# A convolution and two MLPs on one core: second products of two steps together while the weights are decoded

## The chip, the cores and the metric

The kernel runs on one core of a Trainium2 chip. The metric is the device time of one execution in microseconds (us), taken as the median of several runs. Before the change it is 2296.68 us, the median of 3 runs (2296.4 to 2298.99).

## The reference

Three stages over 16384 tokens of 192 channels, cut to what matters:

```python
# x: (4, 4096, 192), 8 heads of 24 channels, a causal convolution of 7 taps per head
w = softmax(weight, axis=-1)
y = einsum('hk,bskhg->bshg', w, windows(x_padded))     # then 16384 x 192
h = y @ w_in1;  g = h * cos(h);         y = g @ w_out1  # 192 -> 2048 -> 192
h = y @ w_in2;  g = where(h > 0, h, exp(min(h, 0)) - 1); out = g @ w_out2
```

The weights of the MLPs come in as 64-bit floats. The kernel reads each as two 32-bit words, low and high, and builds a 32-bit value from them; that is the decoding. Every product is then made from a high and a low part of both factors (h.h, l.h and h.l), so that reduced-precision matmuls give close to single precision.

## The kernel before, in words

**Tiles.** A block is 512 tokens (there are 32), with channels on the partitions. 192 channels are one full set of 128 partitions and one of 64. A step is one block, one MLP (m = 1 or 2) and one index j of 8; it covers 256 of the 2048 hidden channels, as two tiles of 128, i = 0 and 1. There are 512 steps. Blocks go in groups of four: m = 1 over the four blocks (32 steps), then m = 2 over the same four. Blocks 0 and 1 of m = 1 are taken in halves of four steps each, in turn.

**A step's first products (A).** `products_A` (L527) gives 9 matmuls for each of the two tiles of the step; each uses 64 rows of the array. `side_by_side` issues those of the two tiles in turn, so that one works on the upper and one on the lower rows at the same time. The results u go to a ring of four PSUM banks (`ring_bank`, L520): tile t = 2s + i uses bank t mod 4, so step s + 2 writes the banks that step s wrote.

**What becomes of u.** For a tile of m = 1: ScalarE rounds u to an integer (L608), VectorE takes the fraction (L617), ScalarE makes the sine (L623), VectorE multiplies it with u (L631, the last reader of the bank), ScalarE takes the high part gh (L637), GpSimd the low part gl (L644). `step` (L874) writes these in an order by hand: in step s, for t = 2s and then t = 2s + 1, first L608 and L617 of tile t, then L623 and L631 of tile t - 1, then L637 and L644 of tile t - 2, and between them pieces of the decoding, taps of the convolution and evacuations. So L631 of the second tile of step s is issued in step s + 1, behind L608 and L617 of the first tile of step s + 1. Each engine takes its instructions in that order. gh and gl have six buffers each, those of three steps.

**A step's second products (B).** They come LAG = 3 steps later. While the weights are decoded, `whole_B` (L554) makes them as 10 matmuls that use all 128 rows, into two banks, a0 and a1. After that, four banks are free for it and B is made of 20 matmuls of 64 rows, which `products` (L585) issues side by side with those of A. A block keeps the first form when the decoding isn't over at its first B; that is so for the first 32 steps, and their B are issued in steps 3 to 34. PE's order there is A(3) B(0) A(4) B(1) A(5) B(2) and so on.

**Decoding.** The weights of both MLPs come in 30 pieces (`pieces`, L791). Each goes through `decode` (L178) in stages that `advance` (L814) issues: the load into a raw buffer; on ScalarE L195 and for two pieces of three the absolute value, L197; on VectorE L199, for the third piece of three the absolute value instead (L201), then L202 and L203; on GpSimd L205; then the high part on ScalarE and the low part on GpSimd (L233 and L234, or L254 and L255). `need` (L838) issues further stages until what a step's products read is ready. Raw buffers 4 and 5 lie in a tile (`rows`) whose other columns hold the convolution's tap matrices; RAW_FROM says from which step on they may be used.

**The opening.** `opening` (L927) is a generator that runs once after each step. After step 2 it issues the 7 taps of block 2's first 128 channels as matmuls (`conv_by_products`, L398, line L403, into bank a1), ScalarE's copy of them (L940), a transpose on VectorE (L350) and loads. Further taps follow on VectorE, one a step (L376).

Of the kernel before, what the change touches and what calls it, by code (L numbers as in the profile page):

```python
# [12 lines left out]
I32 = mybir.dt.int32  # L13
# [11 lines left out]
PAIR = 4  # L25
AWAKE = 14
AHEAD, AHEAD2 = 6, 5
RAW_FROM = 0, 0, 0, 0, 3, 3
RAW_UNTIL = 9, 13, 23, 30, 15, 15


# [1 line left out]
def conv_then_two_mlps(ctx, tc, x, weight, w_in1, w_out1, w_in2, w_out2, out):  # L33
# [139 lines left out]
        zp = zt.tile([P, 2, N], F32R, tag=f"zp{b % ZN}", name="z")  # L173
        return zp[:, 0], zp[:, 1], zt.tile([P, N], F32R, tag=f"zc{b % ZN}", name="z")

    turn, scalar = deque(("", "e1", "")), deque((0, 1, 1))

    def decode(m, load, n):  # L178

        raw, use = raw_tile(n)
        load(raw)
        yield
        lo, hi = raw[..., 0], raw[..., 1]
        brink.reverse()
        t = brink[0][:, 0:n]
        turn.rotate(-1)  # L190
        w = (op if turn[0] else stage).tile([P, N], F32, tag=turn[0] or "w", name="w")[:, 0:n]
        bits = w.bitcast(I32)
        scalar.rotate(-1)
        size = w if scalar[0] else t
        nc.scalar.activation(out=t, in_=lo.bitcast(U32), func=AF.Copy, scale=2.0 ** -51, bias=2.0)  # L195
        if size is w:
            nc.scalar.activation(out=w, in_=f32(hi), func=AF.Abs)  # L197
        yield
        nc.vector.scalar_tensor_tensor(out=lo, in0=hi, scalar=SIGN, in1=t.bitcast(I32), op0=ALU.bitwise_and, op1=ALU.bitwise_or)  # L199
        if size is t:  # L200
            nc.vector.tensor_scalar(out=t.bitcast(I32), in0=hi, scalar1=~SIGN, scalar2=0, op0=ALU.bitwise_and, op1=ALU.bitwise_or)  # L201
        nc.vector.tensor_scalar(out=t, in0=size, scalar1=2.0 ** -15, scalar2=2.0 ** 17 - 2.0 ** 13, op0=ALU.max, op1=ALU.min)  # L202
        nc.vector.tensor_scalar(out=bits, in0=t.bitcast(I32), scalar1=3, scalar2=0, op0=ALU.logical_shift_left, op1=ALU.bitwise_or)  # L203
        yield
        nc.gpsimd.tensor_tensor(out=bits, in0=bits, in1=lo, op=ALU.add)  # L205
        taken.difference_update(use)
        yield w
# [190 lines left out]
    def conv_by_products(b, o):  # L398


        xT = xTs.pop(("a", b))
        for k in range(K):
            nc.tensor.matmul(o, lhsT=taps[:, k], rhs=xT[:, k * Q:k * Q + N], start=k == 0, stop=k == K - 1)  # L403
            if k == K - 1:
                ys["a", b] = o
            yield
# [130 lines left out]
    def products_B(s, i):  # L537

        m, b, j = steps[s]
        if (m, b) not in acc:  # L540
            acc[m, b] = [bank(k, "acc") for k in ("a0", "b0", "a1", "b1")]
        o, c, p = acc[m, b][i], acc[m, b][2 + i], half[i]
        h, l, sel = (wo[m, n] for n in ("h", "l", "s"))
        ops = []
        for f in (2 * j, 2 * j + 1):
            gh, gl = gs[f"{s} {f % 2}"]
            st, sp = f == 0, f == NF - 1
            for to, w, g, first, final in ((o, l, gh, st, False), (o, h, gh, False, False), (c, sel, gh, st, False), (o, h, gl, False, sp), (c, sel, gl, False, sp)):
                ops.append((to, w[p, f], g[p], first, final))
        if s == total - 1:  # L550
            ops = [ops[n] for n in (2, 4, 7, 0, 1, 9, 3, 5, 6, 8)]
        yield from ops

    def whole_B(s):  # L554

        m, b, j = steps[s]
        begins, stops = (j % (NP // 2) for j in (j, j + 1)) if split_up(m, b) else (j, (j + 1) % NP)
        if not begins:
            acc[m, b] = [bank(k, "acc") for k in ("a0", "a1")]
        o, c = acc[m, b]  # L560
        h, l, sel = (wo[m, n] for n in ("h", "l", "s"))
        (gh0, gl0), (gh1, gl1) = gs[f"{s} 0"], gs[f"{s} 1"]
        f0, f1 = 2 * j, 2 * j + 1
        st, sp = not begins, not stops
        ops = [(o, l, f0, gh0), (o, h, f0, gh0), (c, sel, f0, gh0), (o, l, f1, gh1), (o, h, f1, gh1), (c, sel, f1, gh1), (o, h, f0, gl0), (c, sel, f0, gl0), (o, h, f1, gl1), (c, sel, f1, gl1)]
        for n, (to, w, f, g) in enumerate(ops):
            nc.tensor.matmul(to, lhsT=w[:, f], rhs=g, start=st and n in (0, 2), stop=sp and n >= len(ops) - 2)  # L567
# [6 lines left out]
    def ends_here(m, b, j):  # L574
        return j == NP - 1 or split_up(m, b) and j == NP // 2 - 1

    def side_by_side(*streams):

        for pr in zip_longest(*streams):
            for product in pr:  # L580
                if product:
                    o, lhsT, rhs, first, final = product
                    nc.tensor.matmul(o, lhsT=lhsT, rhs=rhs, start=first, stop=final)  # L583

    def products(s):  # L585
        now, then = 0 <= s < total, 0 <= s - LAG < total
        if then and steps[s - LAG][2] == 0 and not late:
            whole.add(steps[s - LAG][:2])
        if not then or steps[s - LAG][:2] in whole:
            if now:  # L590
                side_by_side(products_A(2 * s), products_A(2 * s + 1))
            if then:
                whole_B(s - LAG)
        elif not now:
            side_by_side(products_B(s - LAG, 0), products_B(s - LAG, 1))
        else:
            streams = products_B(s - LAG, 0), products_B(s - LAG, 1)
            side_by_side(chain(products_A(2 * s), streams[0]), chain(streams[1], products_A(2 * s + 1)))
        if then:
            for i in (0, 1):  # L600
                del gs[f"{s - LAG} {i}"]

    def emit_act1(s):
        m = steps[s // 2][0]
# [269 lines left out]
    def step(s):  # L874
        now = 0 <= s < total
        present[0] = s
        if now:
            m, b, j = steps[s]
            need(m, j + 1, "o", "c")
        finish = iter(())  # L880
        if 0 <= s - LAG < total:
            m, b, j = steps[s - LAG]
            need(m, 2 * j + 2, "oh", "os")
        products(s)
        ends = 0 <= s - LAG < total and ends_here(*steps[s - LAG])
        if ends:
            assert not lazy
            finish = evac(*steps[s - LAG])
        if s in begin_at:
            m, b = begin_at[s]  # L890
            chores.append(begin_split(b) if m == 1 else double_z(b))
        first_mlp = now and steps[s][0] == 1
        for i in (0, 1):
            t = 2 * s + i
            if i:
                next(finish, None)
            if now:
                emit_act1(t)
                emit_mid(t)
            next(finish, None)  # L900
            if 0 <= t - 1 < 2 * total:
                emit_act2(t - 1)
                emit_g(t - 1)
            if not prepared and (s < NP // 2 or i != ends and (s < 12 or not ends and (s % 3 or s > 18))):
                advance()
            if 0 <= t - 2 < 2 * total:
                emit_hi(t - 2)
                emit_lo(t - 2)
            if i:
                next(finish, None)  # L910
            if now and not first_mlp and not ends:
                next(cq, None)
                if i and not first_mlp and steps[s][2] in (4, 6):
                    next(cq, None)
            chore()
        if prepared and not late:
            brief.close()
            top.close()
            late.append(ctx.enter_context(tc.tile_pool(name="ps_s", bufs=1, space=bass.MemoryType.PSUM)))

    total = len(steps)
    def run(gen, n=99):
        for _ in range(n):
            if next(gen, 0) == 0:
                break

    def opening():  # L927

        yield
        fold(1, bank("a1", "y"))  # L930
        upper_split(1)
        run(conv_by_products(1, bank("a0", "y")))
        run(split(1))
        conved.update((0, 1))
        turn_segment("a", 2)
        load_a(3)
        yield
        run(conv_by_products(2, bank("a1", "y")))
        y = kept(2)
        nc.scalar.activation(out=y, in_=ys["a", 2], func=AF.Copy)  # L940
        ys["a", 2] = y
        turn_segment("c", 2)
        load_c(4)
        upper = conv_taps("c", 2, xTs.pop(("c", 2)))
        yield
        yield
        yield
        for s in range(5, 12):
            run(upper, 1)
            yield  # L950
        run(upper)
        moved.add("o")
        conved.add(2)
        yield
        lower = conv("a", 3)
        for _ in range(7):
            run(lower, 1)
            yield
        run(lower)
        conved.add(3)  # L960
        yield
# [79 lines left out]
```

## Time and profile before

| | us |
|---|---|
| median of 3 runs | 2296.68 |
| the profiled execution | 2297.01 |
| its span | 2295.3 |
| PE (TensorE matmul) busy | 2265.7 |
| VectorE busy | 1768.8 |
| ScalarE busy | 1862.8 |
| GpSimd busy | 1253.0 |

The profiled execution's own time is 2297.01 us, 1.7 us more than its span, and 0.33 us over the median. All times inside the trace count from the start of the span. In a row of the trace "[0.56 <-DVE w L631]" means that the engine sat idle for 0.56 us until that instruction of VectorE (DVE) had ended. PE is TensorE, PEld its weight loads, ACT ScalarE, POOL GpSimd.

### The profile page before, as it was taken

What the parts mean: (1) busy time and instruction counts of PE and PEld (TensorE: products, weight loads), DVE (VectorE), ACT (ScalarE), POOL (GpSimd) and SP (SyncE); (2) the same over time, 40 slices, a digit from 0 to 9 for tenths busy, and PEclk for the clock granted to TensorE, in tenths of its full rate; (3) what the DMA queues carried; (4) which work ended last, traced back from release to release, by engine and by line L of the source; (5) the groups of instructions that cost most, each with busy time, mean ns of one, the idle gap of its engine ahead of it and who ended that gap; (6) DMA issues with size and microseconds to landing.
All of it is one profiled execution on the core that took longest, in us unless ns stands there. A gap on an engine that the chain in (4) does not pass through costs nothing.

```text
span 2295.3 us, 49382 instructions
## 1 busy us (share of the span) xinstructions
PE 2265.7 (99%) x19226; PEld 1839.5 (80%) x19226; DVE 1768.8 (77%) x2564; ACT 1862.8 (81%) x3422; POOL 1253.0 (55%) x975
## 2 busy tenths in 40 slices
PE   8999999999999999999999999999999999999998
PEld 5667888888888888888888888888888888888887
DVE  7986977779777897778967798676986779777655
ACT  6877788888888788888788888888788887888886
POOL 5895335763367533674446743576435763367532
PEclk9999999999999999999999999999999999999999
DMA  7222221213211132112221123212221113211111
GB/s 167 81 68 49 51 58 36 46 32 64 49 36 38 32 69 48 40 29 57 52 52 33 24 58 55 47 38 44 45 57 35 46 34 64 42 36 38 26 38 22
DMA packets 292603, 111.43 MB, mean 49 GB/s; under 512 B 245840, under 2 KB 260176, under 8 KB 292368
## 3 DMA queue, kind: packets, MB, share of 16 engines
q1 hardware_dynamic: 290048, 107.42, 22.4%
q8 instruction: 150, 2.46, 0.4%
q10 hardware_dynamic: 2320, 0.85, 0.2%
q14 instruction: 85, 0.70, 0.1%
HBM read 30.09 MB, written 12.58 MB: 19 GB/s over the span
## 4 chain that ended last, share of the span: by engine, by line
PE 89%; DVE 8%; issue 1%; ACT 1%; DMA 1%; POOL 0%; ACTq 0%; DVEq 0%; SPq 0%; POOLq 0%
PE acc L583 45%; PE u L583 42%; DVE y L376 1%; PE acc L567 1%; DVE w L633 1%; DVE w L631 1%; DVE w L617 1%; DVE gl L644 1%; DVE t L202 1%; DVE w L203 0%; DMA raw<-in_moe_w_in_dram 0%; DMA raw<-in_moe_w_out_dram 0%; DVE y L374 0%; DVE raw L199 0%; PE y L403 0%
## 5 line engine op out<-in xcount | busy, mean ns | idle before, releaser
L644 POOL TENSOR_TENSOR gl<-w,gh 128x512 fp32r<-128x512 f32 x768 | 1013.7, 1321 | 1001.8 <-ACT gh L637 640.0
L583 PE MATMUL acc<-gh,wo_hl 64*128 64x512 f32 x3840 | 1174.3, 386 | 0.0
L583 PEld LDWEIGHTS acc<-gh,wo_hl 64*128 64x128 f32 x3840 | 705.3, 184 | 75.8 <-DVE z L697 0.4
L583 PE MATMUL acc<-gh,wo_s 64*128 64x512 f32 x1920 | 740.8, 386 | 0.0
L583 PE MATMUL acc<-gl,wo_hl 64*128 64x512 f32 x1920 | 740.2, 386 | 0.0
L583 PE MATMUL acc<-gl,wo_s 64*128 64x512 f32 x1920 | 740.1, 386 | 0.0
L637 ACT ACTIVATE gh<-w 128x512 fp32r<-128x512 f32 x1024 | 641.2, 626 | 16.2 <-DVE w L633 15.8
L583 PE MATMUL u<-ch,wi_c 64*128 64x512 f32 x2048 | 619.4, 391 | 14.1 <-DVE w L631 11.4
L583 PE MATMUL u<-sh,wi_o 64*128 64x512 f32 x2048 | 611.4, 387 | 0.0
L617 DVE SCALAR_TENSOR_TENSOR w<-u,w 128x512 f32<-128x512 f32 x512 | 352.0, 687 | 251.1 <-ACT w L608 249.1
L633 DVE SCALAR_TENSOR_TENSOR w<-w,u 128x512 f32<-128x512 f32 x512 | 347.8, 679 | 215.1 <-ACT w L625 210.0
L610 ACT ACTIVATE w<-u 128x512 f32<-128x512 f32 x512 | 306.2, 598 | 186.7 <-PE u L583 167.1
L608 ACT ACTIVATE w<-u 128x512 int32<-128x512 f32 x512 | 306.4, 598 | 184.2 <-PE u L583 178.5
L583 PE MATMUL u<-z,wi_o 64*128 64x512 f32 x1536 | 427.4, 386 | 0.0
L583 PEld LDWEIGHTS u<-ch,wi_c 64*128 64x128 f32 x2048 | 364.7, 184 | 71.7 <-DVE w L631 18.9
L583 PEld LDWEIGHTS u<-sh,wi_o 64*128 64x128 f32 x2048 | 368.5, 185 | 40.7
L583 PE MATMUL u<-sl,wi_o 64*128 64x512 f32 x1024 | 387.1, 387 | 0.0
L583 PE MATMUL u<-cl,wi_c 64*128 64x512 f32 x1024 | 386.7, 387 | 0.0
L583 PEld LDWEIGHTS acc<-gh,wo_s 64*128 64x128 f32 x1920 | 353.3, 184 | 37.9 <-DVE e L698 0.3
L583 PEld LDWEIGHTS acc<-gl,wo_hl 64*128 64x128 f32 x1920 | 353.3, 184 | 37.6
L583 PEld LDWEIGHTS acc<-gl,wo_s 64*128 64x128 f32 x1920 | 353.2, 184 | 37.6
L631 DVE TENSOR_TENSOR w<-u,w 128x512 f32<-128x512 f32 x512 | 348.8, 681 | 41.4 <-ACT w L623 41.4
(143 smaller groups left out, 3608.2 us busy)
## 6 DMA issues: line engine op xcount, KB each, us to landing
out_dram<-e SPq DMA_DIRECT2D x189, 64.0 KB, 2.0
xa<-in_x_dram SPq DMA_DIRECT2D x124, 88.0 KB, 2.9
sh<-z SPq DMA_DIRECT2D x64, 128.0 KB, 2.9
sl<-z SPq DMA_DIRECT2D x64, 128.0 KB, 2.5
ch<-z SPq DMA_DIRECT2D x64, 128.0 KB, 2.4
cl<-z SPq DMA_DIRECT2D x64, 128.0 KB, 2.4
sh<-xh SPq DMA_DIRECT2D x62, 128.0 KB, 2.3
sl<-xl SPq DMA_DIRECT2D x62, 128.0 KB, 2.3
```

Of the source, the lines that this page charges most:

```text
L202: nc.vector.tensor_scalar(out=t, in0=size, scalar1=2.0 ** -15, scalar2=2.0 ** 17 - 2.0 ** 13, op0=ALU.max, op1=ALU.min)
L376: nc.vector.scalar_tensor_tensor(out=o, in0=i, scalar=w, in1=o, op0=ALU.mult, op1=ALU.add)
L567: nc.tensor.matmul(to, lhsT=w[:, f], rhs=g, start=st and n in (0, 2), stop=sp and n >= len(ops) - 2)
L583: nc.tensor.matmul(o, lhsT=lhsT, rhs=rhs, start=first, stop=final)
L608: nc.scalar.activation(out=w.bitcast(I32), in_=u, func=AF.Copy, bias=0.25)
L610: nc.scalar.activation(out=w, in_=u, func=AF.Relu, scale=-1.0)
L617: nc.vector.scalar_tensor_tensor(out=w, in0=u, scalar=0.25, in1=w.bitcast(I32), op0=ALU.add, op1=ALU.subtract)
L631: nc.vector.tensor_tensor(out=w, in0=u, in1=w, op=ALU.mult)
L633: nc.vector.scalar_tensor_tensor(out=w, in0=w, scalar=-1.0, in1=u, op0=ALU.add, op1=ALU.max)
L637: nc.scalar.activation(out=gh, in_=wrk[t], func=AF.Copy)
L644: eng.tensor_tensor(out=gl, in0=wrk.pop(t), in1=f32(own[0]), op=ALU.subtract)
```

## The change

Four edits. The B of a step in the first form are no longer issued in each step, but those of two steps together in every other one: `due` gives nothing where s - 3 is even, and steps s - 4 and s - 3 where it is odd. The order on PE becomes A(3) A(4) B(0) B(1) A(5) A(6) B(2) B(3) and so on; the order on the other engines follows the same rule as before. Every absolute value of the decoding is made by ScalarE. Of block 2's taps as matmuls, three are issued after step 2 and four after step 3, with what follows them. Raw buffers 4 and 5 are used from step 4 on instead of step 3.

```diff
-RAW_FROM = 0, 0, 0, 0, 3, 3
+RAW_FROM = 0, 0, 0, 0, 4, 4
...
-    turn, scalar = deque(("", "e1", "")), deque((0, 1, 1))
+    turn = deque(("", "e1", ""))
...
-        scalar.rotate(-1)
-        size = w if scalar[0] else t
         nc.scalar.activation(out=t, in_=lo.bitcast(U32), func=AF.Copy, scale=2.0 ** -51, bias=2.0)
-        if size is w:
-            nc.scalar.activation(out=w, in_=f32(hi), func=AF.Abs)
+        nc.scalar.activation(out=w, in_=f32(hi), func=AF.Abs)
         yield
         nc.vector.scalar_tensor_tensor(out=lo, in0=hi, scalar=SIGN, in1=t.bitcast(I32), op0=ALU.bitwise_and, op1=ALU.bitwise_or)
-        if size is t:
-            nc.vector.tensor_scalar(out=t.bitcast(I32), in0=hi, scalar1=~SIGN, scalar2=0, op0=ALU.bitwise_and, op1=ALU.bitwise_or)
-        nc.vector.tensor_scalar(out=t, in0=size, scalar1=2.0 ** -15, scalar2=2.0 ** 17 - 2.0 ** 13, op0=ALU.max, op1=ALU.min)
+        nc.vector.tensor_scalar(out=t, in0=w, scalar1=2.0 ** -15, scalar2=2.0 ** 17 - 2.0 ** 13, op0=ALU.max, op1=ALU.min)
...
-    def products(s):
-        now, then = 0 <= s < total, 0 <= s - LAG < total
-        if then and steps[s - LAG][2] == 0 and not late:
-            whole.add(steps[s - LAG][:2])
-        if not then or steps[s - LAG][:2] in whole:
+    def is_whole(s):
+        if steps[s][2] == 0 and not late:
+            whole.add(steps[s][:2])
+        return steps[s][:2] in whole
+
+    def due(s):
+
+        if not 0 <= s - LAG < total:
+            return []
+        if not is_whole(s - LAG):
+            return [s - LAG]
+        return [s - LAG - 1, s - LAG] if (s - LAG) % 2 else []
+
+    def products(s, then):
+        now = 0 <= s < total
+        if not then or is_whole(then[0]):
             if now:
                 side_by_side(products_A(2 * s), products_A(2 * s + 1))
-            if then:
-                whole_B(s - LAG)
+            for k in then:
+                whole_B(k)
...
-        if 0 <= s - LAG < total:
-            m, b, j = steps[s - LAG]
+        then = due(s)
+        for k in then:
+            m, b, j = steps[k]
             need(m, 2 * j + 2, "oh", "os")
-        products(s)
-        ends = 0 <= s - LAG < total and ends_here(*steps[s - LAG])
+        products(s, then)
+        ends = bool(then) and ends_here(*steps[s - LAG])
...
-        run(conv_by_products(2, bank("a1", "y")))
+        lower = conv_by_products(2, bank("a1", "y"))
+        run(lower, 3)
+        yield
+        run(lower)
         y = kept(2)
         nc.scalar.activation(out=y, in_=ys["a", 2], func=AF.Copy)
         ys["a", 2] = y
         turn_segment("c", 2)
         load_c(4)
         upper = conv_taps("c", 2, xTs.pop(("c", 2)))
         yield
         yield
-        yield
```

## Rows read from the trace of the kernel before

**Rows 1.** The page, busy time: span; engine, busy us (share), instructions.

```profile
span 2295.3 us, 49382 instructions
PE 2265.7 (99%) x19226; PEld 1839.5 (80%) x19226; DVE 1768.8 (77%) x2564; ACT 1862.8 (81%) x3422; POOL 1253.0 (55%) x975
```

**Rows 2.** Stretches: sum; busy us (x count) of PE, PEld, DVE, ACT, POOL; PEclk, DMA, GB/s.

```profile
44.90:54.48 9.58, 9.58 (x58) 6.82 (x57) 6.23 (x10) 7.22 (x15) 4.26 (x5) 1.00 0.94 215
54.48:101.38 46.90, 42.48 (x226) 29.49 (x225) 45.72 (x69) 40.67 (x76) 44.11 (x34) 0.96 0.35 92
101.38:158.60 57.22, 52.52 (x281) 36.13 (x280) 52.56 (x75) 44.67 (x83) 47.25 (x36) 0.97 0.27 67
158.60:192.79 34.19, 31.02 (x169) 21.41 (x168) 25.59 (x40) 26.63 (x51) 28.61 (x23) 1.00 0.27 70
192.79:221.51 28.72, 28.72 (x169) 20.45 (x169) 16.85 (x24) 20.70 (x39) 17.42 (x15) 1.00 0.24 50
230.00:2290.00 2060.00, 2055.32 (x18118) 1696.44 (x18114) 1578.90 (x2267) 1691.08 (x3093) 1086.05 (x817) 1.00 0.21 44
```

**Rows 3.** PE's waits from 48 to 222 us: total, times, longest.

```profile
PE u L583 <- DVE w L631: 11.4, 13, 1.8
```

**Rows 4.** Timeline, steps 30 and 31: start, length, engine, line, operation, what it waited for.

```profile
197.58 0.73 PE L583 MATMUL u<-ch,wi_c 64*128 64x512 f32 x4
...
199.85 0.73 PE L567 MATMUL acc<-gh,wo_hl 128*128 128x512 f32 x2
200.01 0.60 ACT L608 ACTIVATE w<-u 128x512 int32<-128x512 f32 x1 [1.62 <-PE u L583]
...
200.50 0.62 ACT L623 ACTIVATE w<-w 128x512 f32<-128x512 f32 x1
200.64 0.69 DVE L617 SCALAR_TENSOR_TENSOR w<-u,w 128x512 f32<-128x512 f32 x1 [1.97 <-ACT w L608]
...
201.25 0.68 DVE L631 TENSOR_TENSOR w<-u,w 128x512 f32<-128x512 f32 x1
...
201.81 0.40 PE L567 MATMUL acc<-gl,wo_hl 128*128 128x512 f32 x1
...
202.04 0.40 PE L567 MATMUL acc<-gl,wo_s 128*128 128x512 f32 x1
...
202.36 0.50 PE L583 MATMUL u<-ch,wi_c 64*128 64x512 f32 x2
```

**Rows 5.** Timeline of PE, where it waited longest inside a step's first products.

```profile
54.48 0.50 PE L583 MATMUL u<-ch,wi_c 64*128 64x512 f32 x1
56.75 0.73 PE L583 MATMUL u<-ch,wi_c 64*128 64x512 f32 x3 [1.77 <-DVE w L631]
...
114.12 0.73 PE L583 MATMUL u<-ch,wi_c 64*128 64x512 f32 x3 [1.62 <-DVE w L631]
...
136.10 0.80 PE L583 MATMUL u<-ch,wi_c 64*128 64x512 f32 x3 [1.52 <-DVE w L631]
...
160.80 0.73 PE L583 MATMUL u<-ch,wi_c 64*128 64x512 f32 x3 [1.69 <-DVE w L631]
```

**Rows 6.** Busy time in two stretches of low granted clock; columns as in Rows 2.

```profile
58.00:61.50 3.50, 3.50 (x13) 2.34 (x10) 3.16 (x5) 2.37 (x5) 2.88 (x4) 0.52 0.51 124
136.60:140.00 3.40, 3.40 (x16) 2.17 (x15) 3.40 (x5) 1.17 (x3) 3.10 (x3) 0.50 0.02 5
```

**Rows 7.** Timeline around the opening, steps 2 and 3.

```profile
38.70 6.28 PE L403 MATMUL y<-spare,rows 128*128 128x512 f32 x14 [2.54 <-DVE spare L350]
...
43.57 0.90 DVE L350 STREAM_TRANSPOSE spare<-xc 128x704 f32<-128x704 f32 x1
...
44.90 0.73 PE L583 MATMUL u<-ch,wi_c 64*128 64x512 f32 x4
```

**Rows 8.** Groups of the decoding, 54.48 to 221.51 us: count, busy, mean ns, idle before.

```profile
L197 ACT ACTIVATE w<-raw 128x512 f32<-128x512 f32 x7 | 4.7, 670 | 0.0
...
L201 DVE TENSOR_SCALAR t<-raw 128x512 int32<-128x512 int32 x4 | 2.8, 695 | 0.1
```

More of the change, by code (lines that the diff above doesn't have):

```diff
@@ L583, in side_by_side @@
                     nc.tensor.matmul(o, lhsT=lhsT, rhs=rhs, start=first, stop=final)
-    def products(s):
-        now, then = 0 <= s < total, 0 <= s - LAG < total
-        if then and steps[s - LAG][2] == 0 and not late:
-            whole.add(steps[s - LAG][:2])
-        if not then or steps[s - LAG][:2] in whole:
+    def is_whole(s):
[11 more added lines that the diff above has]
+        if not then or is_whole(then[0]):
             if now:
                 side_by_side(products_A(2 * s), products_A(2 * s + 1))
-            if then:
-                whole_B(s - LAG)
+            for k in then:
+                whole_B(k)
         elif not now:
-            side_by_side(products_B(s - LAG, 0), products_B(s - LAG, 1))
+            side_by_side(products_B(then[0], 0), products_B(then[0], 1))
         else:
-            streams = products_B(s - LAG, 0), products_B(s - LAG, 1)
+            streams = products_B(then[0], 0), products_B(then[0], 1)
             side_by_side(chain(products_A(2 * s), streams[0]), chain(streams[1], products_A(2 * s + 1)))
-        if then:
+        for k in then:
             for i in (0, 1):
-                del gs[f"{s - LAG} {i}"]
+                del gs[f"{k} {i}"]
     def emit_act1(s):
@@ L880, in step @@
         finish = iter(())
-        if 0 <= s - LAG < total:
-            m, b, j = steps[s - LAG]
+        then = due(s)
+        for k in then:
+            m, b, j = steps[k]
             need(m, 2 * j + 2, "oh", "os")
-        products(s)
-        ends = 0 <= s - LAG < total and ends_here(*steps[s - LAG])
+        products(s, then)
+        ends = bool(then) and ends_here(*steps[s - LAG])
         if ends:
```

## The prediction

> **What bounds the kernel now.** I begin with busy time by engine: PE is busy for 99% of the span [rows 1]. That is an average over two very different parts, so next come the stretches [rows 2]. From 230 us on PE is busy for 2055 of 2060 us and nothing in the change touches that part: what is lost or won before 222 us arrives at the end one to one. The change acts only on steps 3 to 34, on PE from 44.90 us, the first product of step 3, to 221.51 us, the first of step 35. I cut them at the first products of steps 5, 13, 23, 29 and 35. In the last stretch (steps 29 to 34) PE has no holes: 28.72 us for six steps, 4.79 us a step. In the three before it PE idles: 46.90 us for 8 steps (5.86 each), 57.22 for 10 (5.72), 34.19 for 6 (5.70). VectorE is busy for 45.72 of 46.90 us and GpSimd for 44.11 in the first of these, VectorE for 52.56 of 57.22 in the second. So the decode steps are held by VectorE, with GpSimd close behind. The table of waits says how PE feels it: it waited 13 times, 11.4 us in all, for L631 [rows 3], the last reader of the PSUM bank that the next first product writes. That is the edge to follow.
>
> **Pairing B: what it saves.** In steps 30 and 31 [rows 4] A takes 199.85 - 197.58 = 2.27 us and B 202.36 - 199.85 = 2.51 us. A is 9 slots (two matmuls of 64 rows at a time), B 10 slots, and the last two of B start 0.23 us apart (201.81, 202.04). So 2.27 - 9 x 0.23 = 0.20 us of A and 2.51 - 10 x 0.23 = 0.21 us of B are no slot. Each change of form therefore costs about 0.2 us. Two steps have four changes now and two afterwards: 0.4 us saved per pair, 16 pairs, some 6 us if nothing else moved.
>
> **Pairing B: what it uncovers.** Now follow the bank. A(s+2) writes the banks of A(s). Its second matmul needs L631 of the second tile of step s, which is written in step s+1 behind L608 and L617 of that step's first tile. So it can't run before A(s+1) has ended and three more instructions have. The timeline shows this chain free of other work [rows 4]: A(30) gives way to B at 199.85; L608 starts at 200.01, L623 (behind it on ScalarE) at 200.50, L617 at 200.64, L631 at 201.25, and it ends at 201.93. That is 2.08 us after A's end; for the handover to PE I add an estimate of 0.06 us, between those of 0.03 us (end of L608, 200.61, to L617) and 0.13 us (end of L623, 201.12, to L631) in these rows, and take 2.14 us. Today B, 2.51 us, lies exactly over it. After the change every even step's A follows directly on an odd step's A, with nothing in between: PE stands for 2.14 us in each pair. Behind that wait on PE's queue are the rest of A and both B, so all of them are late; ScalarE and VectorE in turn wait for A.
>
> A pair (A odd, hole, A even, B, B) is then 2.27 + 2.14 + 2.16 (A from its second matmul, half a slot less) + 2.30 (ten slots) + 2.51 = 11.38 us, say 11.40. Against 2 x 4.79 = 9.57 us where PE alone is the limit: 1.83 us worse per pair. In the decode stretches against 11.73, 11.44 and 11.40 us. The sum over the 15 pairs of steps 5 to 34: 15 x 11.40 = 171.0 against 167.03 us now, **+4.0 us**. It holds if the other engines' work fits into 11.40 us, below.
>
> **The absolute values.** Six L201 lie in these stretches, 0.695 us each ([rows 8] have four of them; the other two are of the same length), three between 54 and 101 us: 2.1 us. VectorE's 45.72 us become 43.6 against 4 x 11.40 = 45.6; the second stretch has 51.2 against 57.0. ScalarE takes six L197 of 0.670 more; its 40.67 become 42.7 in 45.6. So the swap buys room that the hole then takes; its worth on the path is about nothing. If the hole weren't there it would be worth up to 4.2 us. GpSimd keeps its 44.11 us, and with 45.6 available it is the tightest. I count no extra for engines this full; the bound on the other side is 0.5 us in each of the nine decode pairs, +4.5 us.
>
> **The taps.** 14 matmul records of L403 take 6.28 us, 0.90 us a tap [rows 7]. Four taps after A(3) instead of before it: A(3) starts 3.6 us earlier, at 41.3 us. The four taps, 3.6 us, then lie over the 2.14 us chain, so A(4) sees no hole: it starts at 41.4 + 2.27 + 3.6 = 47.2, B(0) and B(1) run from 49.5 to 54.3, and A(5) starts at 54.3 against 54.48. The transpose of 0.90 us moves behind step 3's VectorE work, with the loads that SP issues after it; VectorE starts step 3 some 3.5 us sooner, so both are covered. Worth -0.2 us on PE's clock position; bounds -2 (VectorE's head start lasts) and +1.
>
> **Raw buffers, evacuation, order of the decoding.** Two pieces load a step later; worked through piece by piece, each is still loaded a step or more ahead of its use, and the decoding ends three steps later than before but ahead of step 35. Nothing; if that failed a whole block more would stay in the first form, but there are over three steps of room. An evacuation of a0 and a1 now has a whole A and a hole more before the next B, so it can only be less late. gh and gl are reused right behind the B that reads them: in an even step L637 must wait for the third matmul of the first B, 0.9 us after A, while L608 and L623 in front of it end 1.3 us after A. Nothing.
>
> **The clock.** A hole costs more than its length when the granted clock falls. The timeline has PE's four longest waits of this kind, 1.52 to 1.77 us of idle time [rows 5]. After the ones that ended at 56.75 and 136.10 the clock fell to half, 1.2 GHz, for 3.4 us [rows 6]; after those of 114.12 and 160.80 it stayed at 2.4 GHz. Two in four. A stretch of 3.4 us at half speed loses 1.7 us of matmuls; today most of that vanishes under VectorE's work. My hole, counted as those are (after the one matmul that goes ahead), is some 1.7 us of idle time: the same kind. With two in four, 7 of 15 holes would cost 1.6 us each, as PE, by then the limit, works on through A and two B: **+11 us**. Bounds: none (0) to all (15 x 1.6 = 24 us).
>
> The Trainium skill has this pattern in "TensorE: Matmul & The Clock Gate", section "A second HAM failure mode: psum-queue depth-cycling": a kernel that cycles through PSUM banks idles briefly between groups of matmuls, and the clock swings between its two levels. By it, nearly each hole would be followed by a slow stretch; this trace agrees in two of four.
>
> **The sum.** -0.2 + 4.0 + 11.2 = +15 us: 2297.0 + 15 = 2312 for the profiled execution, and as the median is 0.33 us lower, about 2311.5 us.
>
> **The rivals.**
> 1. *Hole without the clock*: the waits come as worked out, the granted clock stays at its upper level. +4 us, up to +8 with crowded engines: 2301 to 2305. For it: two of the four rows. Chance 0.24.
> 2. *Every hole drops the clock*: 4 + 24 = +28 us, 2325. For it: from the first matmul of A to the second my hole has 2.25 us, as the one that the clock fell after had (54.48 to 56.75, 2.27) [rows 5]. Against it: the two rows without a fall. Chance 0.10.
> 3. *The hole is shorter than it looks, and the change is faster.* Place: the second matmul of every even A; it decides at 1.88 us, where a pair equals the present mean of 167.03 / 15 = 11.14 us. At half, 1.07 us, a pair has 10.33 us; VectorE would hold the first two stretches at 43.6 and 51.2 us, and six pairs make 62.0: 156.8 against 167.0, -10 us, 2286. For it: PE's 13 waits for L631 average 0.9 us. Against it: each of those had a B in front. Chance 0.10.
> 4. *The edits cancel or the pairing does little*: within 4 us either way. Only 32 of 512 steps are touched. Chance 0.08.
>
> **How the numbers follow.** The forecast (holes, with the clock falling after some) has 0.48, the rivals 0.24, 0.10, 0.10 and 0.08. From 2300 to 2326 us the range holds the forecast, nearly all of rivals 1 and 2, and leaves out 3 and 4. About 0.2%, 4.6 us, is what a measurement of this kernel can tell from no change; slower by more is the forecast, rival 2 and most of rival 1: 0.77. Within it: rival 4 and the low end of rival 1, 0.13. Faster: 0.10.
>
> **What would show it.** In the changed kernel PE's waits for L631 between 48 and 226 us should rise from 11.4 us to some 26 us, about 15 of them, in every second A, and with them steps 29 to 34 should take 34 us or more instead of 28.72. The granted clock should be under 0.95 over that stage. L201 is gone, and VectorE's busy share falls below 0.9 there. Step 3's first product stands near 41.3 us. If steps 29 to 34 take under 28.7 us the chain that I read [rows 4] is wrong; if they take 34 and the clock stays at 1.00, the clock term is.

## The result, and the profile after

The changed kernel takes 2320.38 us, the median of 4 runs (2316.46 to 2323.12), against 2297.3 us for the kernel before (4 runs, 2296.4 to 2298.99). The ratio is 1.0098, with a 95% interval of 1.0081 to 1.0116: slower by 23 us. The direction is the one forecast; with 14.8 us predicted, the size was forecast too small. The profiled execution took 2320.98 us, 24.0 us over that of the kernel before.

The line numbers have moved: A is now issued at L578 (it was L583), B at L562 (L567), and the chain behind u is L614, L623, L629, L637, L643 (it was L608, L617, L623, L631, L637). L639 is the last reader of the bank for m = 2.

The page, busy time and granted clock in 40 slices:

```profile
span 2319.3 us, 49394 instructions
...
PE 2271.5 (98%) x19226; PEld 1875.0 (81%) x19226; DVE 1765.9 (76%) x2554; ACT 1866.5 (80%) x3432; POOL 1251.8 (54%) x975
...
PEclk9998999999999999999999999999999999999999
```

The clock row has an 8 in the fourth slice, which the kernel before didn't have. Busy time of the engines by the same cuts, at the first products of steps 5, 13, 23 and 29 (columns as in [rows 2]):

```profile
54.11:103.09 48.98, 41.64 (x226) 30.28 (x226) 42.87 (x63) 39.73 (x75) 42.55 (x33) 0.93 0.39 101
103.09:168.73 65.64, 53.93 (x281) 39.45 (x280) 51.37 (x72) 45.89 (x85) 48.80 (x38) 0.90 0.24 56
168.73:208.53 39.80, 33.47 (x169) 24.41 (x168) 22.10 (x34) 26.51 (x49) 24.67 (x20) 0.87 0.24 64
208.53:245.97 37.44, 31.94 (x169) 23.26 (x168) 19.43 (x27) 21.28 (x39) 18.04 (x15) 0.91 0.18 38
```

The four stretches have grown from 46.90, 57.22, 34.19 and 28.72 us [rows 2] to 48.98, 65.64, 39.80 and 37.44: 24.8 us together, and that covers the whole loss of 24.0 us. Step 35 begins at 245.97 us and not at 221.51. The clock is at 0.87 to 0.93, where it was 0.96 to 1.00. VectorE, which was busy for 97% of the first of these stretches, is busy for 88% of it now, and for 52% of the last (59% before).

PE's waits from 48 to 246 us (total, times, longest):

```profile
PE u L578 <- DVE w L637: 29.1, 14, 3.5
PE u L578 <- DVE w L639: 1.8, 1, 1.8
```

Fifteen waits, one in each pair, 30.9 us in all, where there were 13 of 11.4 us [rows 3]. The row of m = 2 is the last pair's. This idle time of PE, between the first and the second matmul of an even step's A, is called the hole below. The timeline of one of them, between the first products of steps 29 and 30:

```profile
210.72 0.39 PE L578 MATMUL u<-ch,wi_c 64*128 64x512 f32 x1
210.98 0.60 ACT L614 ACTIVATE w<-u 128x512 int32<-128x512 f32 x1 [2.46 <-PE u L578]
211.47 0.62 ACT L629 ACTIVATE w<-w 128x512 f32<-128x512 f32 x1
211.61 0.69 DVE L623 SCALAR_TENSOR_TENSOR w<-u,w 128x512 f32<-128x512 f32 x1 [4.45 <-ACT w L614]
...
212.22 0.68 DVE L637 TENSOR_TENSOR w<-u,w 128x512 f32<-128x512 f32 x1
...
212.96 0.73 PE L578 MATMUL u<-ch,wi_c 64*128 64x512 f32 x3 [1.84 <-DVE w L637]
...
215.22 0.73 PE L562 MATMUL acc<-gh,wo_hl 128*128 128x512 f32 x2
```

Set beside [rows 4], this is the same chain, L614, L629, L623, L637, at the same distances. Only what PE does meanwhile has changed: B used to run there, and now the one matmul at 210.72 goes ahead and PE waits until 212.96, 0.06 us after the end of L637 (212.90).

The opening, PE's timeline:

```profile
38.02 2.84 PE L398 MATMUL y<-spare,rows 128*128 128x512 f32 x6 [2.14 <-DVE spare L345]
40.80 0.73 PE L578 MATMUL u<-ch,wi_c 64*128 64x512 f32 x4
...
43.06 3.70 PE L398 MATMUL y<-spare,rows 128*128 128x512 f32 x8
46.69 0.73 PE L578 MATMUL u<-ch,wi_c 64*128 64x512 f32 x4
...
48.95 0.73 PE L562 MATMUL acc<-gh,wo_hl 128*128 128x512 f32 x2
```

Step 3's first products begin at 40.80 us instead of 44.90 [rows 7], the four taps lie over the chain, and A(4) follows without a wait at 46.69.

Busy time in three stretches of low clock (columns as in [rows 2]):

```profile
71.40:74.90 3.50, 3.50 (x14) 2.33 (x11) 3.43 (x5) 2.77 (x6) 3.37 (x3) 0.51 0.22 66
109.00:112.50 3.50, 3.50 (x12) 2.36 (x9) 3.43 (x5) 3.50 (x8) 3.34 (x3) 0.51 0.32 73
132.80:139.80 7.00, 6.14 (x22) 4.42 (x23) 6.47 (x10) 4.27 (x8) 6.24 (x5) 0.51 0.07 21
```

There are ten such stretches between 71 and 242 us, one of them (132.9 to 139.7) of twice the length of the others. The kernel before had two [rows 6].

### The profile page after: what moved, and what is told of

Read it like the earlier page. It is cut to its first block, busy times and chain, and to the rows that moved or that the text cites. A ratio compares the mean times of both kernels' runs of the same rounds, so it can differ in the third digit from the quotient of the medians.

```text
span 2319.3 us, 49394 instructions
## 1 busy us (share of the span) xinstructions
PE 2271.5 (98%) x19226; PEld 1875.0 (81%) x19226; DVE 1765.9 (76%) x2554; ACT 1866.5 (80%) x3432; POOL 1251.8 (54%) x975
## 3 DMA queue, kind: packets, MB, share of 16 engines
q10 hardware_dynamic: 2320, 0.85, 0.2%
## 4 chain that ended last, share of the span: by engine, by line
PE 91%; DVE 5%; issue 1%; ACT 1%; DMA 1%; POOL 0%; ACTq 0%; SPq 0%; DVEq 0%; POOLq 0%
PE acc L578 45%; PE u L578 43%; PE acc L562 3%; DVE y L371 1%; DVE w L639 1%; DVE gl L650 1%; DVE w L623 1%; DVE w L637 1%; DMA raw<-in_moe_w_out_dram 0%; ACT w L614 0%; DVE y L369 0%; DMA raw<-in_moe_w_in_dram 0%; DVE z L759 0%; ACT gh L643 0%; DVE t L197 0%
## 5 line engine op out<-in xcount | busy, mean ns | idle before, releaser
L578 PE MATMUL acc<-gh,wo_hl 64*128 64x512 f32 x3840 | 1174.2, 386 | 0.0
L578 PEld LDWEIGHTS acc<-gh,wo_hl 64*128 64x128 f32 x3840 | 705.4, 184 | 69.9
L578 PE MATMUL acc<-gh,wo_s 64*128 64x512 f32 x1920 | 740.7, 386 | 0.0
L578 PE MATMUL acc<-gl,wo_hl 64*128 64x512 f32 x1920 | 740.2, 386 | 0.0
L578 PE MATMUL acc<-gl,wo_s 64*128 64x512 f32 x1920 | 740.0, 386 | 0.0
L643 ACT ACTIVATE gh<-w 128x512 fp32r<-128x512 f32 x1024 | 641.2, 626 | 20.5 <-DVE w L639 16.0
L578 PE MATMUL u<-ch,wi_c 64*128 64x512 f32 x2048 | 618.4, 391 | 33.4 <-DVE w L637 29.1
L578 PE MATMUL u<-sh,wi_o 64*128 64x512 f32 x2048 | 615.8, 390 | 0.0
L623 DVE SCALAR_TENSOR_TENSOR w<-u,w 128x512 f32<-128x512 f32 x512 | 352.0, 687 | 270.3 <-ACT w L614 268.1
L639 DVE SCALAR_TENSOR_TENSOR w<-w,u 128x512 f32<-128x512 f32 x512 | 347.8, 679 | 217.6 <-ACT w L631 213.0
L614 ACT ACTIVATE w<-u 128x512 int32<-128x512 f32 x512 | 305.7, 597 | 201.1 <-PE u L578 180.6
L578 PEld LDWEIGHTS u<-ch,wi_c 64*128 64x128 f32 x2048 | 364.8, 184 | 85.5 <-DVE w L637 35.9
L578 PE MATMUL u<-z,wi_o 64*128 64x512 f32 x1536 | 428.7, 387 | 0.0
L578 PEld LDWEIGHTS u<-sh,wi_o 64*128 64x128 f32 x2048 | 370.7, 186 | 38.4
L578 PE MATMUL u<-sl,wi_o 64*128 64x512 f32 x1024 | 389.7, 390 | 0.0
L578 PE MATMUL u<-cl,wi_c 64*128 64x512 f32 x1024 | 387.6, 388 | 0.0
L578 PEld LDWEIGHTS acc<-gl,wo_hl 64*128 64x128 f32 x1920 | 353.3, 184 | 35.0
L578 PEld LDWEIGHTS acc<-gh,wo_s 64*128 64x128 f32 x1920 | 353.3, 184 | 35.0
L578 PEld LDWEIGHTS acc<-gl,wo_s 64*128 64x128 f32 x1920 | 353.2, 184 | 35.0
L637 DVE TENSOR_TENSOR w<-u,w 128x512 f32<-128x512 f32 x512 | 348.7, 681 | 41.9 <-ACT w L629 41.9
```

What stands on the lines that cost most here:

```text
L614: nc.scalar.activation(out=w.bitcast(I32), in_=u, func=AF.Copy, bias=0.25)
L623: nc.vector.scalar_tensor_tensor(out=w, in0=u, scalar=0.25, in1=w.bitcast(I32), op0=ALU.add, op1=ALU.subtract)
L637: nc.vector.tensor_tensor(out=w, in0=u, in1=w, op=ALU.mult)
L639: nc.vector.scalar_tensor_tensor(out=w, in0=w, scalar=-1.0, in1=u, op0=ALU.add, op1=ALU.max)
L643: nc.scalar.activation(out=gh, in_=wrk[t], func=AF.Copy)
```

## The experiments

My theory after the result: the wait for the bank costs 1.8 us a pair and calls down the clock, which costs about as much again; the other edits are small. The rivals are that the fuller ScalarE or the raw buffers cost the time, that the pairing blocks something else (the buffers of gh and gl), or that the clock falls for another reason.

**The hole filled, with nothing else gained.** In the even steps the two tiles' products are issued one after the other:

```diff
-            if now:
+            if now and then:
+                side_by_side(products_A(2 * s))
+                side_by_side(products_A(2 * s + 1))
+            elif now:
                 side_by_side(products_A(2 * s), products_A(2 * s + 1))
```

> The changed kernel, but in the even steps (the ones whose first products follow directly on another step's) the 9 products of the first tile are issued before the 9 of the second, not in turn with them. The first tile's bank is long free, so PE has some 2.1 us of work where it now waits, and the work of the two tiles no longer overlaps: a pair of steps stays at 2.27 + 2.1 + 2.1 + 4.8 = about 11.4 us with PE never idle. Theory (the wait for the bank costs 1.8 us a pair, and the fall of the clock behind it 1.55 us in ten pairs): PE's waits for the last reader of the bank go from 29 us to under 5 us, the granted clock between 60 and 240 us goes to 1.00 but for one or two stretches, and the time is 2301 to 2306 us. Rival (the clock falls because of the order of the forms, or the time goes to the fuller ScalarE): clock and time stay, 2316 us or more.

Measured: 2314.55 us (4 runs, ratio 1.0067, interval 1.0052 to 1.0082). The time lies between the two forecasts; the trace tells which part held. Busy time by stretches, from steps 13, 23 and 29:

```profile
101.66:171.65 69.99, 63.62 (x282) 47.30 (x281) 54.38 (x72) 46.13 (x86) 50.81 (x39) 0.88 0.24 58
171.65:206.09 34.44, 34.30 (x169) 25.58 (x168) 21.97 (x35) 25.25 (x48) 23.58 (x19) 1.00 0.23 62
206.09:240.49 34.40, 34.34 (x171) 25.58 (x170) 19.26 (x27) 21.95 (x41) 18.10 (x15) 1.00 0.19 41
```

and PE's waits:

```profile
PE u L578 <- DVE w L640: 4.8, 4, 4.1
PE u L578 <- DMA sl<-xl: 2.1, 1, 2.1
```

In steps 23 to 34 the kernel did what the theory says: 68.84 us for six pairs, 11.47 each, with the clock at 1.00. The changed kernel has pairs of the same 11.47 us where its clock stays up, but needed 77.2 us for these six. So with the same length of a pair, PE idle in the one and busy in the other, the clock falls in the one alone. That settles the clock term: five falls and one longer hole (0.77 us) make 8.4 us, 1.5 us a fall. What I had missed lies in steps 13 to 22, 69.99 us. There a tap on VectorE took 6.33 us:

```profile
151.17 6.33 DVE L371 SCALAR_TENSOR_TENSOR y<-xT,wch,y 128x512 f32<-128x512 f32 x1
...
158.75 1.22 PE L578 MATMUL u<-ch,wi_c 64*128 64x512 f32 x3 [4.08 <-DVE w L640]
```

Behind it L626 and L640 waited (the chain again), and PE for L640, 4.08 us; the other long wait there, 2.1 us, is for a transfer. In both places the clock was low, for about 10 us after the wait for the transfer and for about 7 us around the other: the stretch has 0.88. The stretch is 12.6 us over five pairs of 11.47. Without these two places the kernel would, by that sum, be at 2302 us, in the range that the theory gave.

**The hole taken away.** In the odd steps the sine and product of the tile before are issued first:

```diff
+            sooner = i == 0 and LAG <= s < total and not then
+            if sooner:
+                emit_act2(t - 1)
+                emit_g(t - 1)
             if now:
                 emit_act1(t)
                 emit_mid(t)
             next(finish, None)
-            if 0 <= t - 1 < 2 * total:
+            if not sooner and 0 <= t - 1 < 2 * total:
```

> The changed kernel, but in the odd steps of the stage the sine and the product of the step before's second tile are issued ahead of the first two operations of this step's first tile, so that they no longer queue behind an operation that waits for this step's products. Theory (the hole is this order in the queues of ScalarE and VectorE, and nothing of the pairing itself): the last reader of the bank ends while PE still works on the second products, the hole is gone in nearly all 15 pairs, the clock stays up, steps 29 to 34 take 3 x 9.3 = 28 us, the decode pairs are held by VectorE and GpSimd at 10.6 to 11.2 us, and the time is 2284 to 2293 us, under both kernels. Rival (pairs of second products hold gh and gl too long with six buffers each, and GpSimd's waits for PE, 19 us in ten waits now, take the hole's place): the time stays over 2303 us with PE waiting for the same line.

Measured: 2296.56 us (10 runs, 2292.79 to 2299.19), ratio 0.9988, interval 0.9978 to 0.9999: 24 us under the changed kernel, and level with the one before; over the upper end of what I had expected by 3.6 us. The profile is of the fastest of the ten runs, 2292.79 us; its waits and stretches (steps 5, 13, 23 and 29 on):

```profile
PE u L578 <- DVE w L637: 17.0, 12, 2.5
```

```profile
53.92:96.86 42.94, 38.51 (x225) 28.72 (x225) 40.81 (x63) 39.64 (x75) 41.88 (x32) 1.00 0.43 114
96.86:155.22 58.36, 50.30 (x281) 36.74 (x281) 50.12 (x72) 45.77 (x85) 50.23 (x39) 0.97 0.25 61
155.22:188.22 33.00, 28.88 (x169) 21.25 (x169) 22.30 (x35) 25.01 (x47) 25.32 (x20) 1.00 0.29 81
188.22:217.71 29.49, 28.36 (x169) 21.19 (x168) 18.57 (x27) 22.98 (x42) 18.28 (x15) 1.00 0.23 48
```

The order of four instructions in two queues gives back the whole loss. The clock is up but for one stretch. The pair of steps 13 and 14 takes 9.11 us (96.86 to 105.97), and there the pairing shows what it saves: 9.57 - 9.11 = 0.46 us, as worked out from the changes of form. But twelve waits for the same line remain, 17.0 us. In the longest, 2.53 us, VectorE still had three operations of the decoding and a tap of 1.12 us between the end of the sine (143.33) and L637 (145.90); for the others no cause is shown. The last stretch, 29.49 us, doesn't even reach the 28.72 us without pairs: of its three pairs the middle one takes 9.11 us, the first 10.05 (a load that ScalarE waited 1.58 us for stands in front of the sine) and the last 10.33 (PE waits 0.71 us for L639, the last reader for m = 2), and a hole has no B over it. The kernel without pairs, below, took 2291.47 us in the same runs. So in this arrangement the pairing gives no gain in this stage, even without the order that made its hole.

**The pairing alone**, on the kernel before (old mix of absolute values, taps all after step 2, raw buffers from step 3).

> The kernel before with the pairing alone: absolute values in the old mix, the taps of block 2 all after step 2, raw buffers 4 and 5 from step 3. Theory: the loss is the pairing's, so the time is that of the changed kernel plus the hole between steps 3 and 4 and the 3.6 us that the split gains: 2320 to 2328 us. Rival (the absolute values on ScalarE lengthen the chain in the hole): under 2312 us.

Measured: 2323.74 us (4 runs), ratio 1.0109, interval 1.0094 to 1.0124. As the theory had it: the loss is there without the other three edits, and the absolute values don't lengthen the hole. Its waits for the bank (total, times, longest), with one more pair that has a hole, that of steps 3 and 4:

```profile
PE u L583 <- DVE w L642: 31.7, 17, 2.8
```

**Everything but the pairing**, with the taps all after step 2:

```diff
-        return [s - LAG - 1, s - LAG] if (s - LAG) % 2 else []
+        return [s - LAG]
```

> The changed kernel without the pairing: second products in each step, the taps of block 2 all after step 2; all absolute values on ScalarE and raw buffers 4 and 5 from step 4 stay. Theory: the wait for the bank is covered by the second products again, VectorE loses six operations of 0.70 us in a stage that it holds: 2293 to 2297 us, no slower than before. Rival (ScalarE's additional work, or raw buffers a step later, is what costs): 2303 us or more.

Measured: 2291.47 us (5 runs), ratio 0.9968, interval 0.9955 to 0.9981, faster than expected by 1.5 us. Stretches (steps 5, 13, 23 and 29 on) and waits:

```profile
54.02:97.59 43.57, 40.85 (x226) 28.18 (x225) 42.06 (x65) 41.41 (x78) 43.19 (x33) 1.00 0.44 121
97.59:151.78 54.19, 50.87 (x281) 35.59 (x281) 47.46 (x70) 41.85 (x78) 47.24 (x36) 1.00 0.22 53
151.78:187.28 35.50, 30.50 (x169) 21.17 (x169) 24.03 (x38) 28.67 (x55) 28.16 (x23) 1.00 0.33 88
187.28:216.10 28.82, 28.82 (x169) 20.91 (x168) 18.64 (x27) 22.27 (x42) 19.08 (x16) 1.00 0.26 58
```

```profile
PE u L578 <- DVE w L637: 9.8, 12, 3.1
```

PE still waits 12 times, but 9.8 us in all, not 31. Against [rows 2] the first stretch is shorter by 3.3 us and the second by 3.0; the third is 1.3 longer. The clock is at 1.00 throughout; the kernel before had two falls. That isn't the same in each execution. The longest wait of this profile, and the wait in the same place in the profile of the same kernel in later runs (the last of the three kernels below), are:

```profile
155.42 0.73 PE L578 MATMUL u<-ch,wi_c 64*128 64x512 f32 x3 [3.14 <-DVE w L637]
```

```profile
155.07 0.73 PE L578 MATMUL u<-ch,wi_c 64*128 64x512 f32 x3 [3.02 <-DVE w L637]
```

After the first the clock stayed at 1.00; after the second it was at 0.51 from 156.4 to 159.8 us. So the length of a wait alone doesn't decide whether the clock falls.

**Which of the remaining edits.** Three kernels in the same runs: the absolute values alone, on the kernel before; the changed kernel with its pairing kept for B(0) and B(1) alone,

```diff
-        return [s - LAG - 1, s - LAG] if (s - LAG) % 2 else []
+        return {LAG: [], LAG + 1: [0, 1]}.get(s, [s - LAG])
```

and the kernel without pairing once more.

> The kernel before with one edit: all absolute values on ScalarE. The kernel without pairing (that edit and raw buffers from step 4) came out near 2291.5 us. Theory: VectorE holds the decode steps as long as second products cover the bank's chain, so ten operations less on it (0.70 us each, 0.43 us for the short pieces) are 4 to 7 us, and the raw buffers a step later are worth nothing: 2290 to 2295 us. Rival (the gain is the raw buffers', which shifts loads away from the first steps): 2296 to 2299 us, no difference from before.

> The changed kernel with the pairing kept for the first two second products alone, where the four taps of block 2 lie between the first products of steps 3 and 4; from step 5 on second products come in each step again. Theory: this keeps what the split brings (first products of step 3 some 3.6 us sooner, VectorE's work starts sooner) without any hole: 1 to 4 us under the kernel without pairing, so 2287 to 2291 us, under the kernel before by over 0.2%. Rival (the split was only needed for the pairing and gains nothing by itself): the time of the kernel without pairing, within 1 us.

> The kernel without pairing once more, to stand beside the other two in the same runs: 2290 to 2293 us by what it measured the first time.

Measured, against 2299.1 us for the kernel before in these runs: the absolute values alone 2290.89 us (10 runs, ratio 0.9968, interval 0.9958 to 0.9978), the first pair alone 2290.37 us (6 runs, 0.9965, 0.9953 to 0.9978), no pairs 2292.7 us (6 runs, 0.9971, 0.9960 to 0.9982). The three can't be told apart. So the gain is that of the absolute values, and the fuller ScalarE isn't what costs; the raw buffers are worth nothing that shows, and for the split of the taps by itself the run is inconclusive: I had expected 1 to 4 us under the kernel without pairs, and the interval allows that as well as no gain. The first three stretches of the absolute values alone (steps 5, 13 and 23 on):

```profile
54.26:97.84 43.58, 40.86 (x226) 28.10 (x225) 42.04 (x66) 41.37 (x78) 43.20 (x33) 1.00 0.38 104
97.84:152.44 54.60, 51.26 (x282) 35.63 (x281) 48.49 (x73) 43.49 (x81) 47.46 (x36) 1.00 0.26 64
152.44:187.05 34.61, 31.69 (x170) 22.52 (x169) 24.89 (x39) 28.68 (x56) 29.57 (x24) 0.95 0.29 78
```

Against [rows 2] the first is shorter by 3.3 us and the second by 2.6; the third is 0.4 longer, with one fall of the clock.

The runs of the first pair go from 2288.31 to 2297.03 us, and the slowest is the profiled one. Its trace has another long tap, and PE's wait behind it:

```profile
123.81 4.74 DVE L371 SCALAR_TENSOR_TENSOR y<-xT,wch,y 128x512 f32<-128x512 f32 x1
...
129.79 0.95 PE L578 MATMUL u<-ch,wi_c 64*128 64x512 f32 x3 [3.79 <-DVE w L637]
```

All three kernels are faster than the kernel before and the changed one, by one edit of this change that the pairing had buried.

## Why the prediction was right

**The hole: right, to 0.1 us.** 2.25 us from the first matmul of A to the second was worked out, and 2.24 measured (210.72 to 212.96). Five pairs had no fall of the clock; they take 11.46 to 11.51 us, and 11.40 was forecast. Fifteen of 11.47 make 172.05 against 167.03 us: +5.0, forecast +4.0.

**The clock: right as a mechanism, too small in its count.** I took two falls in four waits from [rows 5], so 7 of 15. It was 10 of 15, one of them of double length. Take 5.0 us for the holes and 3.2 us for the three longer ones (below) off the 24.8 us, and 16.6 us are left for eleven lengths of slow clock, 1.5 us each, as in the comparison with the tiles in turn. Forecast were 7 of 1.6 us, 11.2. This is the term that was mis-sized: 5.4 of the 9.6 us by which these four stretches were forecast short. The longer holes make 3.2 and the regular ones 1.0; all three terms were short the same way, so none hid another. The rule of the Trainium skill that I weighed it against ("TensorE: Matmul & The Clock Gate", "A second HAM failure mode: psum-queue depth-cycling") has the clock swing between its levels with brief idle times between groups of matmuls: ten of fifteen holes agree with that, five don't. The count lies between the two in four that I took and nearly each.

**Crowded engines: bounded, not counted.** Three holes were longer than the rest. Two of them, with what made them late:

```profile
128.79 3.62 DVE L371 SCALAR_TENSOR_TENSOR y<-xT,wch,y 128x512 f32<-128x512 f32 x1
...
133.66 0.79 PE L578 MATMUL u<-ch,wi_c 64*128 64x512 f32 x2 [3.54 <-DVE w L637]
```

```profile
170.33 0.63 ACT L193 ACTIVATE t<-raw 128x512 f32<-128x512 uint32 x1 [2.53 <-DMA raw<-in_moe_w_out_dram]
...
173.92 0.80 PE L578 MATMUL u<-ch,wi_c 64*128 64x512 f32 x2 [2.60 <-DVE w L637]
```

A tap of 3.62 us kept L623 waiting in the first; a load that ScalarE waited 2.53 us for in the second; a third wait, ending at 160.12, is again of 2.60 us; there a tap of 1.10 us stood in front of L623. Together 1.70 + 0.76 + 0.76 = 3.2 us over the usual 1.84. The bound in the prediction was 4.5 us, and the value taken was nothing; a value between would have been better.

**The absolute values: nothing with the pairs, right; too little without.** With the pairs, the kernel that keeps the old mix has a ratio of 1.0109 and the changed one 1.0098, and their intervals overlap. "If the hole weren't there it would be worth up to 4.2 us" was the step that failed: 0.32% or 7 us were measured. I had counted only the six L201 of these stretches, at their own length. The first stretch alone, with three L201 or 2.1 us, became 3.3 us shorter. The two falls of the clock in the kernel before (0.96 and 0.97 in the first two stretches) weren't in the sum; with the absolute values alone these stretches have 1.00, and one fall comes in the third. How much of the rest the falls make isn't shown.

**The taps and the raw buffers: right.** A(5) begins at 54.11 us; 54.3 was forecast, and it was 54.48 before. **The rivals:** longer pairs without the fall of the clock (2301 to 2305) are what the kernel with the tiles in turn shows in its last six pairs. That pairs would be faster with a shorter hole (2286) fell: with the order that made the hole changed, they come level with the kernel before (2296.56 us).

## What to carry to other kernels

Before two groups of products are put together, ask which chain the work between them covered: here 2.5 us of PE work lay over a chain of 2.1 us on ScalarE and VectorE, and taking it away saved 0.4 us of changes of form and uncovered all of the chain. A hole on PE of some 2 us in every pair can have a second price, the clock, that is larger than the hole: in this case 16.6 us against 5.0, with falls after ten of fifteen holes. Edits made together should be timed apart: one of these was worth 7 us and was buried under a loss of four times that (2291 to 2320 us).

## What the runs showed of the hardware that wasn't expected

A tap on VectorE, a SCALAR_TENSOR_TENSOR with two inputs in SBUF, takes as little as 0.73 us and as much as 3.62 in the changed kernel (instruction, count, shortest, median and longest ns):

```profile
L371 DVE SCALAR_TENSOR_TENSOR y<-xT,wch,y x258: 730/750/3615, 122.6 to 1997.8; 128x512 f32<-128x512 f32 x129
```

and 4.74 and 6.33 us in the two timelines above. In the 6.33 us, from 151.17 to 157.50, GpSimd ran five instructions one after another, until 156.94. Instructions of VectorE with one input in PSUM don't show it: L637 took at most 0.69 us in all its 512 executions in the changed kernel. The Trainium skill says in "SBUF — State Buffer", sections "SBUF: two separate sides" and "Who interferes with whom", that a VectorE instruction with two SBUF inputs contends with a GpSimd instruction that reads SBUF, and that the one that comes second is blocked until the first ends. The taps fit the contention; but here the wait went on over five GpSimd instructions and not one. L196, of the same operation on int32, also with both inputs in SBUF, doesn't fit. It never took more than 0.68 us in the changed kernel, also with GpSimd beside it:

```profile
125.55 1.29 POOL L650 TENSOR_TENSOR gl<-w,gh 128x512 fp32r<-128x512 f32 x1
...
126.75 0.67 DVE L196 SCALAR_TENSOR_TENSOR rows<-rows,t 128x512 int32<-128x512 int32 x1
126.81 1.30 POOL L684 TENSOR_TENSOR z<-rows,z 128x512 fp32r<-128x512 f32 x1
```

No run tried the taps without GpSimd beside them, so what makes a tap long isn't shown.
